# A linear attention in front of a mixture of experts: its instructions held to one fixed sequence

## The chip, the core and the metric

The kernel runs on one core of a Trainium2 chip. The core has five engines that run side by side, each through its own instructions in order: TensorE (PE, matrix multiplies), VectorE (DVE), ScalarE (ACT), GpSimd (POOL) and SyncE (SP), which here only starts DMA transfers. They meet through semaphores. Matrix products land in PSUM (eight banks), everything else lives in SBUF. The metric is the device time of one execution in microseconds (us); lower is better.

## What is computed

The reference is a linear attention followed by a mixture of eight experts with a balanced (Sinkhorn) gate, all in float32:

```python
# attention: q, k, v are (4 batches, 8 heads, 576, 64), omega is (128, 64)
def phi(x):
    proj = einsum('bhsd,md->bhsm', x, omega)
    h = proj - sum(x * x, -1) / 2
    return exp(h - max(h, -1)) / sqrt(m)
q_p, k_p = phi(q * scale), phi(k * scale)
kv, z = einsum('bhsm,bhsd->bhmd', k_p, v), sum(k_p, axis=2)
x = einsum('bhsm,bhmd->bhsd', q_p, kv) / (einsum('bhsm,bhm->bhs', q_p, z)[..., None] + 1e-6)
# experts: x as (2304, 512), w_gate (512, 8), w1 (8, 512, 1024), w2 (8, 1024, 512)
P = exp(x @ w_gate - max);  8 times: rows to sum 1, columns to sum 1, times N / E
out = sum over e of P[:, e] * (relu(x @ w1[e]) @ w2[e])
```

## The kernel before

**Jobs.** The attention is cut into 36 jobs. A job takes half of the heads of 256 rows of a batch's keys or queries; the 64 rows left over in each batch are paired over two batches (`kr`, `qr`). A job transposes its rows (`tp`, copied to `th` by ACT for keys and by DVE for queries), projects them on omega (`pp`, 16 matmuls in the profile), takes the row maximum out of PSUM (DVE, `sqs`), adds the squared norm to it (`cn`), and exponentiates: half of the job by way of DVE and one ACT instruction (`ex<-ex`), the other half by four ACT instructions that take `cn` as bias (`ex<-pp,cn`). A key job then multiplies by the values (`kv`). A query job transposes its features (`qp`, copied to `qt` by ACT), multiplies by `kvs` (`np`), divides (`rd`, `xt`, DVE), and its rows become token tiles by another transpose (`xp`, copied to `xf` by ACT). The squared norms come from an ACT square (`sq`) and a tree of sums on POOL (`squares`, two buffers).

**Side work between the jobs.** When six token tiles (a chunk, three in all) are there, `token_operands` computes the gate logits (`lp`, `gp`) and seven operands `xs` of a Strassen product: sums on POOL (on DVE for the last chunk), a rounded copy by ACT, a residual by DVE, and a DMA that writes both to DRAM (`xd`). `xs` has a ring of four tiles. The first expert's weights are loaded by `stage` and cut by `split` into a rounded half `wh` (ACT) and a residual `wl`, in the attention on POOL.

**The order.** The program's text gives the work to a scheduler, which runs a timeline of its own and orders each engine's queue by it. A `tick` advances every job in flight by one stage. `ensure_loads` starts a value's load two jobs ahead and a key's or query's five; SP's queue takes all DMAs. To keep squares, staging and splits from being scheduled too early, eight columns of their buffers are first written by a POOL copy from the newest `cn` (`last_cn`), so that the real write has to wait for it. After the attention, the expert part runs `first` (hidden products, `hx`, `hz`) and `second` (output products, `x`, `z`, `w`) interleaved; the last chunk's operands are the first that it uses.

Of the kernel before, what the change touches and what calls it, by code (L numbers as in the profile page):

```python
# [22 lines left out]
def moe_attention_kernel(  # L23
# [67 lines left out]
    ORDER = [1, 5, 6, 3, 7, 2, 4]  # L91

# [6 lines left out]
    def token_operands(c, x):  # L99
# [7 lines left out]
        next(gate_steps)  # L107

        def sub(o, a, b):
            (nc.vector if last else nc.gpsimd).tensor_tensor(o, a, b, op=ALU.subtract)  # L110

        for i in ORDER:
            if i == 5:
                sub(q(0, 0), q(0, 1), q(0, 0))
            elif i == 6:
                sub(q(0, 0), q(1, 1), q(0, 0))
            elif i == 7:
                sub(q(0, 1), q(1, 1), q(0, 1))  # L120
            elif i == 4:
                sub(q(0, 0), q(1, 0), q(0, 0))
            o = {3: q(1, 1), 7: q(0, 1), 2: q(1, 0)}.get(i, q(0, 0))
# [45 lines left out]
    last_cn = []  # L169
# [14 lines left out]
    def split(u, w, i):  # L184
# [39 lines left out]
        wt[u, w, i] = (hi, lo)  # L224

# [32 lines left out]
    def load(which, key):  # L258
# [31 lines left out]
    def squares(which, key):  # L290
# [5 lines left out]
        if last_cn:  # L296
            nc.gpsimd.tensor_copy(s.rearrange("p h j d -> p (h j d)")[:, :8], last_cn[-1])
# [18 lines left out]
    def feature_stages(which, key, hh, on_act):  # L316


# [10 lines left out]
        yield  # L329
        hs = sqt[which, key].rearrange("p h j t -> p (h j) t")[:, 8 * hh : 8 * hh + 8]  # L330
# [45 lines left out]
    def k_job(key, hh):  # L376
        ex = yield from feature_stages("k", key, hh, True)
        vt = rawt["v", key]
        if key[0] == "r":

            for a in range(2):
                b, r = 2 * key[1] + a, slice(a * SR, (a + 1) * SR)
                for hg in range(2):
# [4 lines left out]
                    if a == 0:  # L388
                        kv_close(b, hg)
# [19 lines left out]
    def q_job(key, hh, t0):
        ex = yield from feature_stages("q", key, hh, True)  # L410
        qt = []
        for g in range(2):
# [3 lines left out]
            t = sc.tile([P, 4, P], F32, tag="qt", bufs=4, name="qt")  # L416
            nc.scalar.copy(t.rearrange("p a s -> p (a s)"), tp)
            qt.append(t)
        yield
        shared = key[0] == "r"  # L420
        nj = 1 if shared else 2
        if hh == 0:
            xts[key] = sc.tile([P, 2, H, D], F32, tag="xt", bufs=2, name="xt")
        xt = xts[key]
        rd = sc.tile([P, 2, 4, 1], F32, tag="rd", bufs=2, name="rd")
        nums = []
        for g in range(2):
            nps = bank("np")
            n3 = nps[:, : 4 * (D + 1)].rearrange("p (h d) -> p h d", h=4)
            nums.append(n3)  # L430
            for i, (h, j) in enumerate(slots(key, hh, g)):
                for a in range(2):
# [3 lines left out]
                        n3[r, i, :], lhsT=qt[g][:, i, r], rhs=kv[:, h], start=True, stop=True  # L436
                    )
            nc.vector.tensor_scalar_add(rd[:, g], n3[:, :, :1], 1e-6 * M)
        nc.vector.reciprocal(rd, rd)
        for g, n3 in enumerate(nums):  # L440
            o = xt[:, 0, g::2] if shared else xt[:, g, 4 * hh : 4 * hh + 4]
            nc.vector.tensor_tensor(o, n3[:, :, 1 : D + 1], rd[:, g].to_broadcast([P, 4, D]), op=ALU.mult)
        yield
        if not shared and hh == 0:
            return
        c, col = t0 // CT, t0 % CT * P
        if c not in xf:
            xf[c] = sc.tile([P, KD, CL], F32, tag="xf", bufs=2, name="xf")
        for j in range(nj):
            xps = bank("xp")  # L450
            xj = xt[:, j].rearrange("p h d -> p (h d)")
            for kk in range(KD):
                nc.tensor.transpose(xps[:, kk * P : (kk + 1) * P], xj[:, kk * P : (kk + 1) * P], ident)
# [399 lines left out]
```

## Time and profile before

| | us |
|---|---|
| median of 3 runs (1633.61 to 1635.28) | 1633.7 |
| the profiled execution's own time | 1634.42 |
| its span, first to last instruction | 1632.6 |
| busy PE, DVE, ACT, POOL in the span | 1584.5, 1379.9, 777.3, 312.4 |
| mean granted clock of PE | 0.994 |

The span is what the engines' rows cover, and the execution's own time lies some 2 us above it. PE's weight loads (PEld) run beside its matmuls and are counted apart. A granted clock of 1.00 is 2.4 GHz; a mean below it holds some time at 1.2 GHz. Times in the rows below count from the span's start.

### The profile page before, as it was taken

The page shows a single profiled execution, that of the slowest core. Times are in us where ns is not written, and L with a number is a line of the kernel's source. Part 1 is how long each engine was busy: PE and PEld are TensorE (multiplying, and loading weights), DVE is VectorE, ACT ScalarE, POOL GpSimd, SP SyncE. Part 2 cuts the span into 40 slices and gives each one's busy share as a digit, 9 for nine tenths or more (in the row PEclk, how much of TensorE's full clock was granted, in tenths as well). Part 3 has the DMA queues.
Part 4 walks back from the last instruction along what each step waited for, and adds up shares of the span by engine and source line. Part 5 has one row for each costly group of instructions (what it writes and reads, how often), then busy time and mean ns, then how long its engine had stood idle before and what let it go on. Part 6 is the DMA issues. An engine that isn't in the chain of part 4 may idle for free.

```text
span 1632.6 us, 31484 instructions
## 1 busy us (share of the span) xinstructions
PE 1584.5 (97%) x12318; PEld 1551.6 (95%) x12318; DVE 1379.9 (85%) x2714; ACT 777.3 (48%) x1396; POOL 312.4 (19%) x340
## 2 busy tenths in 40 slices
PE   7899799999999999999999999999999999999998
PEld 5778699999999999999999999999999999999997
DVE  3788888998888898989888888989898888889777
ACT  5788654544434444534444444434344444444333
POOL 5585230111111010201111111102011111110003
PEclk9999999999999999999999999999999999999999
DMA  9442866666656565666565665656666556655562
GB/s 237 122 157 73 329 246 216 216 208 218 201 195 213 186 221 198 222 204 232 204 219 197 203 217 179 229 193 229 203 220 218 205 197 206 213 178 192 181 226 77
DMA packets 105315, 329.80 MB, mean 202 GB/s; under 512 B 14800, under 2 KB 43984, under 8 KB 105168
## 3 DMA queue, kind: packets, MB, share of 16 engines
q1 hardware_dynamic: 105168, 327.79, 59.5%
q8 instruction: 98, 1.61, 0.4%
q14 instruction: 49, 0.40, 0.1%
HBM read 306.53 MB, written 21.23 MB: 201 GB/s over the span
## 4 chain that ended last, share of the span: by engine, by line
PE 86%; DVE 7%; ACT 2%; POOL 2%; DMA 2%; issue 1%; SPq 0%; DVEq 0%; ACTq 0%; POOLq 0%
PE hx L549 24%; PE x L650 23%; PE hz L549 18%; PE z L650 11%; PE w L650 6%; PE pp L335 2%; DVE out L676 1%; DVE sm L586 1%; POOL sq L302 1%; DVE bl L586 1%; DVE sqs L338 1%; PE kv L360 1%; DVE xs L126 1%; ACT ex L348 0%; DMA xs<-xd 0%
## 5 line engine op out<-in xcount | busy, mean ns | idle before, releaser
L549 PE MATMUL hx<-xs,wh 128*128 128x384 f32 x1536 | 374.3, 337 | 2.0 <-ACT xs L125 1.4
L676 DVE SCALAR_TENSOR_TENSOR out<-x,prob,out 128x256 f32<-128x256 f32 x497 | 233.3, 476 | 65.8 <-PE x L650 64.3
L549 PE MATMUL hz<-xs,wh 128*128 128x384 f32 x1152 | 281.5, 336 | 2.1 <-ACT xs L125 1.1
L549 PEld LDWEIGHTS hx<-xs,wh 128*128 128x128 f32 x1536 | 270.1, 189 | 3.5 <-issue 3.2
L190 POOL TENSOR_TENSOR st<-st 128x512 f32<-128x512 f32 x80 | 131.7, 1646 | 700.1 <-DVE wl L223 697.1
L549 PEld LDWEIGHTS hz<-xs,wh 128*128 128x128 f32 x1152 | 202.4, 188 | 2.9 <-issue 1.3
L549 PE MATMUL hx<-xs,wl 128*128 128x384 f32 x768 | 199.4, 337 | 0.0
L628 ACT ACTIVATE bh<-hr 128x512 fp32r<-128x512 f32 x144 | 91.2, 634 | 222.0 <-PE x L650 217.0
L676 DVE SCALAR_TENSOR_TENSOR out<-z,prob,out 128x256 f32<-128x256 f32 x252 | 120.0, 476 | 58.0 <-PE z L650 57.2
L222 ACT CAST wh<-st 128x512 fp32r<-128x512 f32 x176 | 105.1, 621 | 110.9 <-PE hx L549 44.8
L624 ACT CAST sh<-sm 128x512 fp32r<-128x512 f32 x144 | 89.7, 623 | 139.9 <-PE z L650 100.1
L549 PE MATMUL hz<-xs,wl 128*128 128x384 f32 x576 | 150.1, 335 | 0.0
L549 PEld LDWEIGHTS hx<-xs,wl 128*128 128x128 f32 x768 | 138.9, 189 | 0.0
L586 DVE SCALAR_TENSOR_TENSOR sm<-hr,sm 128x256 f32<-128x256 f32 x288 | 133.5, 464 | 2.7
L223 DVE TENSOR_TENSOR wl<-st,wh 128x512 fp32r<-128x512 f32 x169 | 119.7, 719 | 11.6 <-ACT wh L222 11.1
L586 DVE SCALAR_TENSOR_TENSOR bl<-hr,bh 128x512 fp32r<-128x512 f32 x144 | 118.2, 821 | 3.1 <-ACT bh L628 1.5
L650 PE MATMUL z<-wh,sh 128*128 128x256 f32 x576 | 117.9, 281 | 2.8 <-ACT sh L607 2.7
L650 PE MATMUL x<-wl,sh 128*128 128x256 f32 x576 | 118.4, 282 | 0.0
L650 PE MATMUL x<-wh,sh 128*128 128x256 f32 x576 | 117.3, 284 | 0.7 <-DVE out L676 0.6
L598 ACT ACTIVATE ah<-hr 128x256 fp32r<-128x256 f32 x144 | 60.3, 419 | 120.6 <-PE x L650 98.9
L650 PE MATMUL z<-wh,sl 128*128 128x256 f32 x576 | 115.5, 282 | 1.6 <-DVE sl L608 1.6
L650 PE MATMUL z<-wl,sh 128*128 128x256 f32 x576 | 116.8, 281 | 0.0
(153 smaller groups left out, 3481.6 us busy)
## 6 DMA issues: line engine op xcount, KB each, us to landing
xs<-xd SPq DMA_DIRECT2D x329, 768.0 KB, 4.4
st<-in_moe_w_dram SPq DMA_DIRECT2D x64, 512.0 KB, 4.9
xd<-xs SPq DMA_DIRECT2D x21, 768.0 KB, 3.8
k<-in_k_dram SPq DMA_DIRECT2D x8, 512.0 KB, 6.5
v<-in_v_dram SPq DMA_DIRECT2D x8, 512.0 KB, 6.5
q<-in_q_dram SPq DMA_DIRECT2D x8, 512.0 KB, 6.2
out_dram<-out SPq DMA_DIRECT2D x32, 128.0 KB, 1.9
kr<-in_k_dram SPq DMA_DIRECT2D x4, 128.0 KB, 6.4
```

What stands on the lines that cost most here:

```text
L126: nc.vector.tensor_tensor(t[:, 1], o, raw(t[:, 0]), op=ALU.subtract)
L190: nc.gpsimd.tensor_tensor(o, a, b, op=op)
L222: nc.scalar.copy(hi, o)
L223: (nc.vector if u > 0 or (w == 2 and i in (1, 6, 7, 4)) else nc.gpsimd).tensor_tensor(lo, o, raw(hi), op=ALU.subtract)
L335: nc.tensor.matmul(pp[g][:, i * M : (i + 1) * M], lhsT=th[r, i], rhs=omt[r], start=True, stop=True)
L549: nc.tensor.matmul(pb, lhsT=a[:, k, g * P : (g + 1) * P], rhs=x[:, b, k, :], start=i in (1, 5, 2) and j == 0, stop=j == len(prods) - 1, sk ...
L586: nc.vector.scalar_tensor_tensor(o, in0=a, scalar=0.0, in1=b, op0=ALU.max, op1=op)
L598: nc.scalar.activation(ah, a11, AF.Relu)
L624: nc.scalar.copy(sh, sm)
L628: nc.scalar.activation(bh, a[:, 1:], AF.Relu)
L650: nc.tensor.matmul(pb, lhsT=ops[s][i][a][:, f], rhs=wt[u, 2, i][b][:, f], start=bool(start) and j == 0, stop=j == len(prods) - 1, skip_gro ...
L676: nc.vector.scalar_tensor_tensor(o, in0=pb, scalar=p, in1=o, op0=ALU.mult, op1=ALU.add)
```

## The change

The attention is written as one sequence. `feature_stages`, `k_job` and `q_job`, generators that the old `tick` advanced, become small functions (`transposes`, `projections`, `maxima`, `shifts`, `exps`, `keys_by_values`, `query_transposes`, `query_copy`, `numerators`, `quotients`, `token_transposes`, `token_copy`) that the new `tick(j)` calls in one order for the jobs j + 1, j, j - 1 and j - 2. What it traces is collected, and at the end every instruction gets an ordering edge (without a semaphore) to the one before it on its engine; SP's DMAs are among them. The expert part gets no edges. The copies from `last_cn` are gone. Loads are asked for eight jobs ahead, in order of use, and a value three jobs later than its key. The token operands of chunks 0 and 1 and the first weight splits follow written plans, a part each half tick (`s` is a sum, `c` a cast, `l` a residual); the sums of chunk 1 go into value buffers that are free by then, no longer over the tokens, and the first weights' residuals `wl` move from POOL to DVE. The first weights are staged at job 7 instead of 16, the second at job 32 instead of 30, the shared query job `qr(0)` goes from the middle to the end, `kvs` has 4 buffers instead of 3, `qr` 2 instead of 1 and `ex` 6 instead of 8. No arithmetic is added to the attention or the experts. The diff, cut to its core:

```diff
@@ token_operands @@
+        if c == 0:
+            at = {i: {3: q(1, 1), 7: q(0, 1), 2: q(1, 0)}.get(i, q(0, 0)) for i in ORDER}
+            plan = "|c1 |c3 l1.s5|c2 l3|c5 l2.s7| l5.s6|c7 |c6 l7| l6.s4| |c4 | l4|"
+        else:
+            at = {1: q(0, 0), 3: q(1, 1), 2: q(1, 0)}
+            for n, i in enumerate((5, 6, 7, 4)):
+                at[i] = vts[n].rearrange("p h c -> p (h c)")[:, : 2 * HL].rearrange("p (k t) -> p k t", k=2)
+            plan = "|s5.c1.c3 s7.l1|c2 l3.s6|c5 l2.s4|c7 l5|c6 l7|c4 l6.l4|"
...
@@ stage, split, squares @@
-            if u == 0:
-                nc.gpsimd.tensor_copy(t[:, 0, 0, :8], last_cn[-1])
...
-        if u == 0 and w == 1:
-            nc.gpsimd.tensor_copy(hi[:, 0, :8], last_cn[-1])
...
-        if last_cn:
-            nc.gpsimd.tensor_copy(s.rearrange("p h j d -> p (h j d)")[:, :8], last_cn[-1])
@@ first_splits (new) @@
+        for step in "|s5.c1 | l1|c2 |c5 l2| l5.s6.s7| |c4 |c6 l4|c7 l6.s3| l7| |c3 | l3|".split():
+            for part in step.split("|"):
+                for what in part.split(".") if part else ():
...
+                    if what[0] == "s":
+                        a, b, op = sums[i]
+                        nc.gpsimd.tensor_tensor(at[i], a, b, op=op)
+                    elif what[0] == "c":
...
+                        nc.scalar.copy(hi, at[i])
+                        wt[0, 1, i] = (hi, lo)
+                    else:
+                        hi, lo = wt[0, 1, i]
+                        nc.vector.tensor_tensor(lo, at[i], raw(hi), op=ALU.subtract)
+                yield
@@ the driver @@
     def ensure_loads(i):
-        for it in list(need):
-            if it[0] <= (i + 2 if it[1] == "v" else i + 5):
-                need.remove(it)
-                load(it[1], it[2])
...
+        while need and need[0][0] <= i + 8:
+            _, w, key = need.pop(0)
+            load(w, key)
...
+    def tick(j):
...
+        now, nxt = job(j), job(j + 1)
+        while closing:
+            kv_close(*closing.pop(0))
+        if now:
+            projections(now)
+            maxima(now, 0)
+        ensure_squares(j)
+        if nxt:
+            transposes(nxt)
+        tps = []
+        if job(j - 1, "q"):
+            tps = query_transposes(job(j - 1))
+            for t in tps:
+                query_copy(job(j - 1), *t)
+        if now:
+            maxima(now, 1)
+            shifts(now)
+            exps(now, 1)
+        go_on()
+        for xt, i, t in turned[: 1 if j < 28 else None]:
+            turned.pop(0)
+            token_copy(token_transposes(xt, i, t), t)
+        if now:
+            exps(now, 0)
+        for it in leftover:
+            next(it, None)
+        leftover.clear()
+        if job(j - 2, "q"):
+            numerators(job(j - 2))
+        if job(j - 1, "k"):
+            it = keys_by_values(job(j - 1))
+            next(it)
+            leftover.append(it)
+        if job(j - 2, "q"):
+            quotients(job(j - 2))
+        go_on()
...
+    in_order = mybir.DependencyInfo(mybir.DependencyClass.NoSync, mybir.DependencyReason.DATA)
+    before = {}
+    for ins in pinned:
+        if ins.engine in before:
+            tc.add_manual_dep(ins, before[ins.engine], in_order, reason="order of the attention")
+        before[ins.engine] = ins.name
```

**The first jobs.** ACT's queue from job 0's exponentials on, before and with the change (the numbers tell buffers apart; `sq_218` is the square of the keys that jobs 5 and 7 use):

```order
L348 ACTIVATE ex_163<-pp_147,cn_158 128x128 x4
L298 ACTIVATE sq_177<-kr_112 128x512
L351 ACTIVATE ex_160<-ex_160 128x512
L326 COPY th_215<-tp_210 128x512
L348 ACTIVATE ex_205<-pp_189,cn_200 128x128 x4
L298 ACTIVATE sq_218<-k_115 128x1024
L351 ACTIVATE ex_202<-ex_202 128x512
```

```order
L419 ACTIVATE ex_171<-pp_140,cn_168 128x128 x4
L415 ACTIVATE ex_170<-ex_170 128x512
L377 COPY th_196<-tp_191 128x512
L419 ACTIVATE ex_202<-pp_181,cn_199 128x128 x4
L415 ACTIVATE ex_201<-ex_201 128x512
L349 ACTIVATE sq_239<-kr_111 128x512
L377 COPY th_254<-tp_249 128x512
```

Each square stood between a job's four exponentials and its last one; it now stands behind the last one. POOL's queue at the start, before and with the change (the last row of before is a copy from `cn`):

```order
L302 TENSOR_TENSOR sq_117<-sq_117 128x16x4
L302 TENSOR_TENSOR sq_127<-sq_127 128x16x32
L302 TENSOR_TENSOR sq_117<-sq_117 128x16x2
L302 TENSOR_TENSOR sq_127<-sq_127 128x16x16
L303 TENSOR_TENSOR sqs_118<-sq_117 128x16
L302 TENSOR_TENSOR sq_127<-sq_127 128x16x8
L304 TENSOR_SCALAR sqs_118<-sqs_118 128x16
L302 TENSOR_TENSOR sq_127<-sq_127 128x16x4
L297 COPY sq_177<-cn_158 128x8
```

```order
L353 TENSOR_TENSOR sq_122<-sq_122 128x16x4
L353 TENSOR_TENSOR sq_122<-sq_122 128x16x2
L354 TENSOR_TENSOR sqs_123<-sq_122 128x16
L355 TENSOR_SCALAR sqs_123<-sqs_123 128x16
L353 TENSOR_TENSOR sq_150<-sq_150 128x16x32
L353 TENSOR_TENSOR sq_150<-sq_150 128x16x16
```

The second tree ran inside the first one; it now follows it, and the copies from `cn` are gone.

**Chunk 0's operands.** DVE's queue around jobs 22 to 24, before and with the change (`xs` are the residuals of token operands, `wl` one of the weights):

```order
L126 TENSOR_TENSOR xs_1705<-xf_834,xs_1705 128x768
L338 TENSOR_REDUCE sqs_1254<-pp_1674 128x4
L126 TENSOR_TENSOR xs_1786<-xf_834,xs_1786 128x768
L338 TENSOR_REDUCE sqs_1254<-pp_1675 128x4
L328 COPY th_1701<-tp_1696 128x512
L126 TENSOR_TENSOR xs_1879<-xf_834,xs_1879 128x768
L126 TENSOR_TENSOR xs_1942<-xf_834,xs_1942 128x768
L340 TENSOR_REDUCE cn_1686<-sqs_1254 128x8
L338 TENSOR_REDUCE sqs_1308<-pp_1749 128x4
L350 TENSOR_TENSOR ex_1688<-pp_1674,cn_1686 128x512
L126 TENSOR_TENSOR xs_2029<-xf_834,xs_2029 128x768
```

```order
L123 TENSOR_TENSOR xs_1549<-xf_833,xs_1549 128x768
L399 TENSOR_REDUCE sqs_1272<-pp_1743 128x4
L379 COPY th_1759<-tp_1754 128x512
L399 TENSOR_REDUCE sqs_1272<-pp_1744 128x4
L404 TENSOR_REDUCE cn_1776<-sqs_1272 128x8
L406 TENSOR_TENSOR ex_1778<-pp_1743,cn_1776 128x512
L123 TENSOR_TENSOR xs_1646<-xf_833,xs_1646 128x768
L276 TENSOR_TENSOR wl_1692<-t_842,wh_1691 128x512
```

Five residuals stood within one and a half jobs; now one stands behind each job's `ex`, and a `wl` joins some of them. The query copy `th` goes from behind both maxima to between them.

**The handover.** PE's queue at the first output products (`ah` and `sh` are their left operands), before and with the change:

```order
L650 MATMUL x<-wh,al 128x256 x2
L650 MATMUL z<-wh,sh 128x256 x2
L650 MATMUL z<-wl,sh 128x256 x2
L467 MATMUL mt<-ident,m_3071 1x128
L650 MATMUL z<-wh,sl 128x256 x2
L650 MATMUL x<-wh,sh_2952 128x256 x2
L549 MATMUL hx<-xs,wh 128x384 x2
```

```order
L751 MATMUL x<-wh,al 128x256 x2
L650 MATMUL hx<-xs,wh 128x384 x2
L650 MATMUL hx<-xs,wl 128x384 x2
L650 MATMUL hx<-xs,wh 128x384 x4
L650 MATMUL hx<-xs,wl 128x384 x2
L650 MATMUL hx<-xs,wh 128x384 x2
L751 MATMUL z<-wh,sh 128x256 x2
```

The twelve `hx` products that came after `sh` now come ahead of it.

## Rows read from the trace of the kernel before

**Rows 1.** By stage: us, busy us of PE PEld DVE ACT POOL, PEclk, DMA, GB/s.

```profile
7.57:48.88 41.31, 32.18 (x477) 27.46 (x477) 20.75 (x42) 25.62 (x62) 25.32 (x58) 0.96 1.11 230
48.88:93.99 45.11, 42.13 (x700) 36.99 (x697) 36.17 (x88) 38.16 (x96) 27.32 (x66) 1.00 0.34 95
93.99:121.76 27.77, 24.82 (x322) 20.81 (x319) 24.18 (x46) 22.43 (x47) 24.70 (x27) 0.88 0.56 210
121.76:157.08 35.32, 33.55 (x533) 29.63 (x533) 29.87 (x76) 29.56 (x77) 18.08 (x36) 1.00 0.18 62
157.08:175.73 18.65, 13.84 (x187) 9.79 (x187) 13.00 (x29) 13.05 (x26) 7.28 (x4) 1.00 0.52 208
175.73:208.00 32.27, 25.03 (x130) 23.04 (x131) 26.32 (x39) 18.12 (x32) 11.29 (x7) 0.89 0.80 320
208.00:1610.00 1402.00, 1395.30 (x9856) 1388.15 (x9855) 1215.04 (x2373) 620.18 (x1045) 185.23 (x121) 1.00 0.61 207
```

**Rows 2.** Waits of ACT, 0 to 50 us: us in total, times, longest.

```profile
ACT sq L298 <- POOL sq L297: 5.5, 4, 1.6
ACT sq L298 <- DMA k<-in_k_dram: 1.9, 1, 1.9
```

**Rows 3.** Timeline of PE: start, us, engine, line, operation [idle before <-releaser].

```profile
25.42 1.69 PE L360 MATMUL kv<-v,ex 128*64 128x65 f32 x32 [2.43 <-ACT ex L351]
...
53.75 1.15 PE L435 MATMUL np<-kvs,qt 128*64 128x65 f32 x32
54.74 1.10 PE L360 MATMUL kv<-v,ex 128*64 128x65 f32 x32
55.77 1.16 PE L335 MATMUL pp<-omt,th 64*128 64x128 f32 x16
56.86 0.66 PE L323 MATMUL tp<-ident,q 128*128 128x128 f32 x4
...
109.61 1.16 PE L335 MATMUL pp<-omt,th 64*128 64x128 f32 x8 [1.28 <-DVE th L328]
...
173.48 0.63 PE L453 MATMUL xp<-ident,xt 128*128 128x128 f32 x4 [2.13 <-DVE xt L442]
...
198.53 0.51 PE L650 MATMUL z<-wh,sh 128*128 128x256 f32 x2 [2.67 <-ACT sh L607]
```

**Rows 4.** Timeline of ACT, 23 to 25 and 67 to 70 us.

```profile
23.79 1.06 ACT L298 ACTIVATE sq<-q 128x1024 f32<-128x1024 f32 x1 [1.44 <-POOL sq L297]
...
67.24 1.16 ACT L348 ACTIVATE ex<-pp,cn 128x128 f32<-128x128 f32 x4
68.25 0.67 ACT L351 ACTIVATE ex<-ex 128x512 f32<-128x512 f32 x1
68.77 0.62 ACT L326 COPY th<-tp 128x512 f32<-128x512 f32 x1
```

**Rows 5.** Timeline of POOL, 5 to 25 us.

```profile
6.89 2.99 POOL L302 TENSOR_TENSOR sq<-sq 128x512 f32<-128x512 f32 x4 [5.13 <-ACT sq L298]
...
19.66 3.32 POOL L302 TENSOR_TENSOR sq<-sq 128x512 f32<-128x512 f32 x5 [1.17 <-ACT sq L298]
...
23.37 0.27 POOL L304 TENSOR_SCALAR sqs<-sqs 128x16 f32<-128x16 f32 x1
```

**Rows 6.** Timeline of DVE, 13, 94 and 109 us.

```profile
13.51 0.18 DVE L340 TENSOR_REDUCE cn<-sqs 128x8 f32<-128x24 f32 x1 [2.54 <-POOL sqs L304]
...
94.74 0.96 DVE L126 TENSOR_TENSOR xs<-xf,xs 128x768 fp32r<-128x768 f32 x1 [0.15 <-ACT xs L125]
...
109.48 3.84 DVE L126 TENSOR_TENSOR xs<-xf,xs 128x768 fp32r<-128x768 f32 x2
```

**Rows 7.** The page's costliest groups, weight residuals: count | busy, mean ns.

```profile
L223 DVE TENSOR_TENSOR wl<-st,wh 128x512 fp32r<-128x512 f32 x169 | 119.7, 719 | 11.6 <-ACT wh L222 11.1
```

**Rows 8.** Groups of DVE by form, 0 to 176 us.

```profile
L126 DVE TENSOR_TENSOR xs<-xf,xs 128x768 fp32r<-128x768 f32 x13 | 17.5, 1361 | 4.8 <-ACT xs L125 4.7
```

**Rows 9.** The chain that ended last, 174 to 205 us: start, us, what.

```profile
184.66 5.20 DMA xd<-xs
```

More of the change, by code (lines that the diff above doesn't have):

```diff
@@ L106, in token_operands, with total, cast, low @@
         gate_steps = logits(c, x)
[L107 to L123, printed above, removed]
+        if last:
+            next(gate_steps)
+        def total(o, i, s):
+            eng = nc.vector if last else nc.gpsimd
+            a, b = {5: (q(0, 1), s), 6: (q(1, 1), s), 7: (q(1, 1), q(0, 1)), 4: (q(1, 0), s)}[i]
+            eng.tensor_tensor(o, a, b, op=ALU.subtract)
+        def cast(i, o):
             t = token_tile()
             nc.scalar.copy(t[:, 0], o)
+            return t
+        def low(i, o, t):
             nc.vector.tensor_tensor(t[:, 1], o, raw(t[:, 0]), op=ALU.subtract)
@@ L128, in token_operands @@
             nc.sync.dma_start(out=xdram[c, i], in_=raw(t))
-            if last:
+        if last:
+            for i in ORDER:
+                n = len(traced)
+                o = {3: q(1, 1), 7: q(0, 1), 2: q(1, 0)}.get(i, q(0, 0))
+                if i in (5, 6, 7, 4):
+                    total(o, i, o)
+                t = cast(i, o)
+                low(i, o, t)
+                pinned.extend(traced[n:])
                 xop[0, c, i] = t
@@ L314, in slots, with transposes @@
         return [(4 * hh + i, g) for i in range(4)]
-    def feature_stages(which, key, hh, on_act):
+    def transposes(jb):
+        which, key, hh = jb[:3]
         tin = rawt[which, key].rearrange("p h j d -> p (h j d)")
@@ L403, in k_job, with query_transposes @@
         if last:
-            kv_close(b, hh)
+            closing.append((b, hh))
         yield
+    closing = []
     xts = {}
[L409 to L412, printed above, removed]
+    def query_transposes(jb):
+        ex = exs.pop(jb)
+        tps = []
+        for g in (1, 0):
             tp = bank("qp")
@@ L447, in q_job, with token_transposes @@
+    turned = []
+    def token_transposes(xt, j, t):
+        c = t // CT
         if c not in xf:
             xf[c] = sc.tile([P, KD, CL], F32, tag="xf", bufs=2, name="xf")
[L449 to L453, printed above, removed]
-            cs = slice(col + j * P, col + (j + 1) * P)
-            nc.scalar.copy(xf[c][:, :, cs], xps.rearrange("p (k s) -> p k s", k=KD))
-            yield
@@ L457, in q_job, with token_copy @@
-        done_q[c] += nj
-        if done_q[c] == CT:
-            yield from token_operands(c, xf[c])
+        xps = bank("xp")
+        xj = xt[:, j].rearrange("p h d -> p (h d)")
+        for kk in range(KD):
+            nc.tensor.transpose(xps[:, kk * P : (kk + 1) * P], xj[:, kk * P : (kk + 1) * P], ident)
+        return xps
+    def token_copy(xps, t):
+        c, col = t // CT, t % CT * P
+        nc.scalar.copy(xf[c][:, :, col : col + P], xps.rearrange("p (k s) -> p k s", k=KD))
+        done_q[c] += 1
+        if done_q[c] == CT:
+            it = token_operands(c, xf[c])
+            if c < NCH - 1:
+                next(it)
+                extra.append(it)
+            else:
+                at_last.append(it)
@@ L462, in sinkhorn @@
+    extra, at_last = [], []
     def sinkhorn():
@@ L758, in moe_attention_kernel @@
+    begin = len(traced)
+    ensure_loads(0)
+    ensure_squares(-1)
+    for i in range(-1, len(jobs)):
+        if i == 7:
+            stage(0, 1)
+            prepare_gate()
+        if i == 12:
+            it = first_splits()
+            next(it)
+            extra.append(it)
+        if i == 32:
             stage(0, 2)
-        gen = k_job(jb[1], jb[2]) if jb[0] == "k" else q_job(*jb[1:])
-        active.append((jb, gen))
-        tick()
+        tick(i)
         ensure_loads(i + 1)
-    tick()
+    for i in range(len(jobs), len(jobs) + 3):
+        tick(i)
```

179 lines of the change are left out of this document (110 added, 69 removed).

## The prediction, made before the run

> **What bounds the kernel now.** I read the busy time by stage first [rows 1]. From 208 to 1610 us, the expert part, TensorE (PE) is busy 1395.3 of 1402.0 us, and the change pins nothing there. What can move is the attention and the handover before 208 us. I cut them at starts of projections (`pp`, one group of 16 matmuls per job, 36 jobs): A is jobs 0 to 8 (41.31 us), B jobs 9 to 20 (45.11), C jobs 21 to 25 (27.77), D jobs 26 to 34 (35.32), E from the last job's projections to the first expert matmul (18.65), F from there to 208 us (32.27). PE is busy for 93% of B, but 78% of A, 89% of C at a mean granted clock of 0.88, 74% of E, and 78% of F at 0.89 (below 1.00 means that part of the stretch ran at 1.2 instead of 2.4 GHz). So the losses sit in A, C, E and F; B shows what an undisturbed mix of jobs costs, 3.76 us per job.
>
> Why A is slow shows in the waits of the first 50 us [rows 2] and in the engines' rows. ScalarE (ACT) stood 5.5 us, four times, behind the 8-column copies on GpSimd (POOL) that tie a square's buffer to the newest `cn`. The square stands ahead of the exponential that `kv` needs: the square at 23.79 waited 1.44 us, and the `kv` behind it made PE wait 2.43 us until 25.42 [rows 3, 4]. Earlier, POOL ran four of the first square's sums, then began the second square's tree inside the first's, so that the first `cn` waited for POOL until 13.51 [rows 5, 6]. C is slow because the seven token operands of chunk 0 were issued nearly together: two `xs` residuals on VectorE (DVE) took 3.84 us at 109.48, the query copy that PE needed came just ahead of them and late, and PE waited 1.28 us until 109.61 [rows 3, 6]; after that the clock fell.
>
> **The change, term by term.** PE's own sequence hardly changes (in both orders: project, transpose the next job, then query transposes or numerators and `kv`), so what is priced is when ACT, DVE and POOL let it go on.
>
> *A, jobs 0 to 8.* One tree alone takes 4.0 us (from 19.66 to the end of the row at 23.37), so one that starts at 6.89 ends at 10.9, and `cn` comes at 10.95 instead of 13.51 [rows 5, 6]. I keep the slow PE durations of the first two jobs as they are and move job 2 forward by 1.5 us, the part of these 2.5 that PE, itself busy with jobs 0 and 1, can use: it projects at 16.4 (17.9 before). A key job then costs PE, by its row 0.66 (`tp`) and by the steps between starts 1.03 (`kv`) + 1.09 (`pp`), together 2.8 [rows 3], and ACT 1.01 + 0.52 + 0.62 = 2.15 (four exponentials, one more, `th`), with a square of 1.06 3.2 [rows 4]. Every second or third tick has a square; with a hop or two I take 3.1 for each of jobs 2 to 4, so job 5 projects at 25.7. Jobs 5 to 8 cost PE 2.8, 3.8, 2.8 and 3.8 (numerators 0.99, query transposes taken at the same), together 13.2, and 0.4 for hops: job 9 at 39.3, and A is 31.7 us long. I take 33, a gain of 8.3. Bounds: 4 (only most of the 5.5 us of [rows 2] comes back) and 9.6 (the walk as it stands).
>
> *B, jobs 9 to 20.* Most of the first weight splits are now cast here, and their residuals move from POOL to DVE. DVE gains 5 of the 7 inside B at 0.72 each [rows 7], 3.6 us, and goes from 36.17 to 40; ACT gains about 6 casts at 0.62, the row of a copy of the same 128x512 [rows 4], 3.7 us, and goes from 38.16 to 42; PE has 42.13 [rows 1]. They are hidden while each engine stays within PE's time, but with little slack left. I take 46, a loss of 0.9; bounds 43 and 49. The query copy moved between the two maxima costs nothing; it frees PE earlier. The 1 MB of first weights is issued at job 7 instead of 16 and stands ahead of later keys, values and queries in the only queue; those are asked for eight jobs ahead, some 25 us, and 512 KB takes 2.3 us at A's 230 GB/s [rows 1], so I cost it at nothing. If that cover failed it would be the 4.6 us of the two loads.
>
> *C, jobs 21 to 25.* At full clock PE's work is about 24.82 - 0.12 x 27.77 = 21.5 [rows 1]. Of six token residuals of 1.36 [rows 8], four stay at about 1.2, spread over ticks, and two `wl` come: DVE 24.18 - 8.2 + 4.8 + 1.4 = 22.2. I take 22.8, for two engines at that level: a gain of 5.0. Bounds 2 (spread, but the clock still falls) and 6.
>
> *D, jobs 26 to 34.* Here work arrives: three residuals of chunk 0 and one or two of chunk 1 (DVE 29.87 + 5 x 1.2 = 36), and chunk 1's gate logits with some token transposes come over, about 2.5 of the 13.84 us of PE work in E (PE 33.55 + 2.5 = 36) [rows 1]. I take 38.5, a loss of 3.2; bounds 35 and 42.
>
> *E, from the last projections to the first expert matmul.* The chain is maxima, shift, exponentials, query transposes, copies, numerators, quotients, token transposes, their copy, gate logits. Before, DVE had residuals in pairs ahead of the quotients, and PE waited 2.13 us for `xt` until 173.48 [rows 3]. The order now lets one through per step, and two jobs are still in flight behind the last. Without the second residual of each pair I get 15.5, a gain of 3.1; bounds 13 and 18.65 (nothing).
>
> *F, the handover.* Chunk 1's writes begin earlier and no longer stand between chunk 2's: the chain shows 5.20 us for such a write ahead of a cast [rows 9]. PE also stood 2.67 us for `sh` until 198.53 [rows 3]; the new order has twelve `hx` matmuls in that place, about 2.1 us. I take 29.5, a gain of 2.8; bounds 27 and 34 (the same DVE chain, reached with the ring of four `xs` tiles fuller).
>
> *Expert part.* The scheduler reorders it in detail, with nothing added or removed: 0, give or take 1.5.
>
> A rule bears on the residuals. Measured first: one took 0.96 us at 94.74 and two took 3.84 at 109.48 [rows 6], while POOL ran sums. The Trainium skill ("SBUF — State Buffer", "Who interferes with whom") says that a VectorE instruction with two SBUF inputs and a GpSimd instruction that reads SBUF exclude each other for the whole instruction. These rows agree with it. By that rule a residual that meets POOL work doubles, and the seven that move from POOL to DVE would meet the squares' trees; that is the second rival.
>
> Sum: 8.3 - 0.9 + 5.0 - 3.2 + 3.1 + 2.8 = 15.1. The profiled execution took 1634.4 us (its span is 1632.6), 0.7 above the median of 1633.7: 1634.4 - 15.1 = 1619.3, or 1618.6 against the median. I say **1619**.
>
> **Rivals.**
> 1. *The start is bound by loads.* For: the DMA engines' share was 1.11 throughout A [rows 1]. Against: ACT waited only 1.9 us for a key load in the first 50 us [rows 2]. Were it so, A would give 2 instead of 8.3: 1625. Chance 0.10.
> 2. *Residuals held up by POOL.* If 21 residuals took 1.9 instead of 1.2 or 0.72, DVE would have some 19 us more; after my sum B, C and D leave DVE about 10 us of slack, so 8 or 9 end on the path: 1627. For: the pair at 109.48 [rows 6]. Against: POOL loses its seven `wl` and the tie copies, and was busy for only 18.08 of the 35.32 us of D [rows 1]. Chance 0.13.
> 3. *More than I count.* F keeps the clock up, pairs in B lose their waits for `ex`, and all terms come out near their upper bounds: 1608. Chance 0.12.
> 4. *The change doesn't do what it says.* PE's sequence was nearly this one already; if the new order of ACT and DVE only trades waits, the time is within 3 us of 1634. Chance 0.07.
> 5. *Slower.* The fixed order ties ACT into a ring with PE: last exponential of a query job, query transposes and copy, key exponentials, square, `th` copy, query exponentials. By [rows 3, 4] that is 0.5 (half the transposes) + 0.6 + 1.0 + 0.5 + 1.06 + 0.6 + 1.0 + 0.5 = 5.8 us per pair of jobs, up to 2 us of casts and token copies stand in it, and B's pair takes 7.5. If hops add 1.5 us, a pair takes 9.0, and the 13 pairs of B to D lose 20 us, against 15 won: 1639. It decides from a pair of 8.7 us on. For: an ACT that waits now holds up everything behind it. Against: before, pairs ran at 7.5 us with the same copies ahead of the same exponentials. Chance 0.08.
>
> **How the numbers follow.** My forecast (its own range 1613 to 1625) has 0.50. A difference of 0.2%, 3.3 us, is about what a measurement of this kernel can tell from no change. Faster by more: 0.50 + 0.10 + 0.13 + 0.12 = 0.85; the same 0.07; slower 0.08. The range 1610 to 1631 leaves out the fourth and fifth rivals and the far half of the third, 0.2 in all.
>
> **What the new profile would show.** The projections of job 9 near 41 us (48.88 before), of job 21 near 87 (93.99), of job 26 near 109 (121.76), of job 35 near 148 (157.08), the first expert matmul near 163 (175.73), PE steady from some 193 (208). No square that waits for POOL in the first 50 us; token residuals of 0.96 to 1.3 us, one per tick; PE's clock at 1.00 from job 21 to 26. I am wrong if ACT waits for query transposes on every second job, if pairs in B exceed 7.8 us, or if the last chunk's casts still wait some 5 us for writes of `xs`.

## The result, and the profile after

The changed kernel takes 1614.0 us (median of 4 runs, 1611.28 to 1614.47), the kernel before 1633.7 beside it: a ratio of 0.9875, 95% interval 0.9858 to 0.9892, some 20 us less. I had forecast 1619. The profiled execution of the changed kernel (1611.28, span 1609.4) lies 2.7 us below its median and that of the kernel before 0.7 above its own, so the stages below add up to 23.2 us, 3.5 more than the medians differ by; that much is luck.

The stages of the new profile, cut at the same projections as in [rows 1] (the sixth row covers as long a stretch behind the first expert matmul as F did). Columns as there.

```profile
7.54:38.47 30.93, 28.84 (x477) 24.80 (x477) 20.62 (x41) 24.20 (x60) 22.67 (x50) 1.00 0.93 215
38.47:80.51 42.04, 41.24 (x699) 36.71 (x696) 38.65 (x96) 40.05 (x99) 27.70 (x49) 1.00 0.65 152
80.51:101.64 21.13, 20.22 (x343) 16.87 (x339) 18.94 (x39) 19.23 (x46) 14.44 (x20) 1.00 0.35 113
101.64:140.73 39.09, 36.90 (x542) 30.85 (x539) 37.14 (x85) 34.48 (x84) 27.04 (x37) 1.00 0.54 184
140.73:154.87 14.14, 10.93 (x164) 7.84 (x160) 11.58 (x31) 10.44 (x21) 1.54 (x1) 1.00 0.61 245
154.87:187.14 32.27, 26.21 (x141) 24.23 (x142) 26.38 (x37) 17.79 (x32) 10.97 (x7) 0.95 0.85 333
```

| stage | before | forecast | after | gain, forecast | gain, measured |
|---|---|---|---|---|---|
| A | 41.31 | 33 | 30.93 | 8.3 | 10.4 |
| B | 45.11 | 46 | 42.04 | -0.9 | 3.1 |
| C | 27.77 | 22.8 | 21.13 | 5.0 | 6.6 |
| D | 35.32 | 38.5 | 39.09 | -3.2 | -3.8 |
| E | 18.65 | 15.5 | 14.14 | 3.1 | 4.5 |
| first expert matmul to the end | 1456.87 | 1454.1 | 1454.53 | 2.8 | 2.3 |
| sum | | | | 15.1 | 23.2 |

PE is now busy in 93% of A and 98% of B. ScalarE's waits of the first 50 us hold no square that waits for POOL any more, as [rows 2] did:

```profile
ACT th L377 <- PE tp L374: 4.0, 3, 2.1
ACT L289 <- DMA om<-in_omega_dram: 3.3, 1, 3.3
ACT qt L492 <- PE qp L485: 1.9, 3, 1.2
ACT ex L419 <- DVE cn L404: 1.6, 3, 1.1
```

PE's rows that answer to [rows 3], from its timeline (start, us, what, and the wait before it):

```profile
11.34 2.08 PE L389 MATMUL pp<-omt,th 64*128 64x128 f32 x16 [0.68 <-ACT th L377]
...
15.63 1.16 PE L389 MATMUL pp<-omt,th 64*128 64x128 f32 x16
...
152.70 0.63 PE L544 MATMUL xp<-ident,xt 128*128 128x128 f32 x4 [1.38 <-DVE xt L528]
...
179.27 0.50 PE L751 MATMUL z<-wh,sl 128*128 128x256 f32 x2 [1.68 <-DVE sl L709]
180.80 0.51 PE L751 MATMUL x<-wh,sh 128*128 128x256 f32 x2 [1.03 <-ACT wh L246]
182.04 0.80 PE L751 MATMUL x<-wl,sh 128*128 128x256 f32 x2 [0.73 <-DVE wl L247]
```

The reader is to see that job 2 projects at 15.63 (17.9 before) and that the wait of 2.67 us for `sh` in the handover is gone. The wait for `sl` is not new; the kernel before had it behind that for `sh` (its waits of PE, 175 to 208 us):

```profile
PE z L650 <- DVE sl L608: 1.6, 1, 1.6
```

The waits for `wh` (1.03) and `wl` (0.73) behind it are new.

### The profile page after: what moved, and what is told of

It is laid out like the page before. It is cut to its first block, busy times and chain, and to the rows that moved or that the text cites. A ratio compares the mean times of both kernels' runs of the same rounds, so it can differ in the third digit from the quotient of the medians.

```text
span 1609.4 us, 31434 instructions
## 1 busy us (share of the span) xinstructions
PE 1574.7 (98%) x12318; PEld 1543.1 (96%) x12318; DVE 1388.4 (86%) x2721; ACT 774.8 (48%) x1396; POOL 298.1 (19%) x304
## 4 chain that ended last, share of the span: by engine, by line
PE 86%; DVE 10%; ACT 2%; POOL 1%; issue 1%; DMA 0%; SPq 0%; DVEq 0%; ACTq 0%
PE hx L650 24%; PE x L751 23%; PE hz L650 18%; PE z L751 12%; PE w L751 6%; DVE sm L687 2%; DVE out L777 2%; PE pp L389 1%; DVE bl L687 1%; DVE sqs L399 1%; DVE wl L247 1%; POOL sq L353 1%; DVE sl L726 1%; PE tp L374 1%; DVE xs L123 1%
## 5 line engine op out<-in xcount | busy, mean ns | idle before, releaser
L216 POOL TENSOR_TENSOR st<-st 128x512 f32<-128x512 f32 x79 | 126.3, 1598 | 702.6 <-DVE wl L247 698.1
L246 ACT CAST wh<-st 128x512 fp32r<-128x512 f32 x172 | 102.9, 620 | 104.6 <-PE hx L650 43.9
L687 DVE SCALAR_TENSOR_TENSOR sm<-hr,sm 128x256 f32<-128x256 f32 x288 | 137.1, 476 | 2.6
L751 PE MATMUL x<-wh,sl 128*128 128x256 f32 x576 | 117.2, 282 | 0.0
```

Of the source, the lines that this page charges most:

```text
L216: nc.gpsimd.tensor_tensor(o, a, b, op=op)
L687: nc.vector.scalar_tensor_tensor(o, in0=a, scalar=0.0, in1=b, op0=ALU.max, op1=op)
L751: nc.tensor.matmul(pb, lhsT=ops[s][i][a][:, f], rhs=wt[u, 2, i][b][:, f], start=bool(start) and j == 0, stop=j == len(prods) - 1, skip_gro ...
```

## The experiments

Stages are named as above; each run's time is a median of four or five, with a kernel before timed beside it at 1634.2 to 1634.6, and its stages are those of its profiled execution.

**e1: no edges.**

```diff
-    for ins in pinned:
+    for ins in []:
```

> The changed kernel without its ordering edges: same text, same plans, same buffers, but the scheduler orders each queue. Theory of the fixed order (the edges themselves let TensorE run its stream without waits): stages A to E give back most of the 20.8 us they won, A over 35 us (30.9 with edges), B near 45 (42.0), and the time is 1626 to 1634. Rival, the pieces (ties gone, plans, more buffers, earlier loads do it, and the edges only write down what the scheduler would do anyway): A 31 to 32, B 42 to 43, time 1613 to 1617.

Measured: 1657.9 us, ratio 1.0147 (1.0133 to 1.0161): slower than the kernel before by 24 us. A 60.0, B 44.7, C 27.5, D 44.7, E 14.6. Both theories had it wrong in size: the text without its edges is not even the kernel before. ScalarE's and GpSimd's timelines show why A is so long:

```profile
29.57 0.62 ACT L272 CAST wh<-st 128x512 fp32r<-128x512 f32 x1 [6.53 <-DMA st<-in_moe_w_dram]
...
31.28 1.27 POOL L268 TENSOR_TENSOR t<-st 128x512 f32<-128x512 f32 x1 [4.34 <-DMA st<-in_moe_w_dram]
```

The scheduler put casts and sums of the first weights, meant for job 12 on, ahead of exponentials and trees of the first jobs, and both engines stood until that load had landed.

**e2: the kernel before without the ties of its squares.**

```diff
-        if last_cn:
-            nc.gpsimd.tensor_copy(s.rearrange("p h j d -> p (h j d)")[:, :8], last_cn[-1])
```

> The kernel before with one thing taken out: the eight-column copies on GpSimd that tie each square's buffer to the newest cn. If the ties are what made the start slow (ScalarE stood 5.5 us behind them, four times), A falls from 41.3 to 36 to 38 us and the time to 1629 to 1631. Rival, the place of the square (between a job's four exponentials and its last one) and the mixing of two trees on GpSimd cost it: A stays at 40 to 42 and the time at 1632 to 1636.

Measured: 1647.3 us, ratio 1.0083 (1.0069 to 1.0096); A 54.7 (41.3 with the ties). Neither theory foresaw that. ScalarE's timeline:

```profile
34.14 1.06 ACT L296 ACTIVATE sq<-k 128x1024 f32<-128x1024 f32 x1 [7.62 <-DMA k<-in_k_dram]
...
41.12 1.06 ACT L296 ACTIVATE sq<-k 128x1024 f32<-128x1024 f32 x1 [2.93 <-POOL sqs L301]
```

Squares of later jobs now stand ahead of this job's exponentials and wait for loads and trees. ScalarE waited 5.5 us behind the ties [rows 2], and without them A is 13.4 us longer.

**e5: the new text with the old ties, without edges.** The edges out as in e1, and:

```diff
+            if u == 0:
+                nc.gpsimd.tensor_copy(t[:, 0, 0, :8], last_cn[-1])
...
+                        nc.gpsimd.tensor_copy(hi[:, 0, :8], last_cn[-1])
...
+        if last_cn:
+            nc.gpsimd.tensor_copy(s.rearrange("p h j d -> p (h j d)")[:, :8], last_cn[-1])
```

> The changed kernel's text and plans without the ordering edges, but with the eight-column GpSimd copies of the kernel before back on the squares, the first weights' tiles and their rounded halves. The run without edges and without ties took 1657.9 us, with A at 60.0. If the ties alone hold the squares back well enough and the new text and plans bring the rest (theory of the pieces): A 31 to 34, B 42 to 43, time 1613 to 1620. If the edges are what pays (theory of the fixed order), this is the kernel before with small changes: A 37 to 42, B 44 to 46, time 1628 to 1638.

Measured: 1642.3 us, ratio 1.0056 (1.0044 to 1.0069); A 41.0, B 50.4, D 46.5. The plans, buffers and early loads without the order cost 8 us; with it they come with a gain of 20. The theory of the pieces is out.

**e8 and e9: edges on some engines.**

```diff
     for ins in pinned:
+        if ins.engine != mybir.EngineType.Activation:
+            continue
         if ins.engine in before:
```

That is e8; e9 has `if ins.engine not in (mybir.EngineType.Activation, mybir.EngineType.Pool)` in its place.

> The changed kernel with ordering edges on ScalarE's instructions alone; the other engines' queues are the scheduler's. If it is ScalarE's order (squares, copies, casts among the exponentials) that pays, A is 31 to 33 and the time 1613 to 1620. If GpSimd's or VectorE's order counts as much (trees mixed into each other, residuals ahead of maxima), A is 35 to 45 and the time 1622 to 1640.

> The changed kernel with ordering edges on ScalarE and GpSimd alone. With edges on ScalarE alone, GpSimd stood 10.6 us before a sum of the first weights whose load had not landed, with the trees of the squares behind it, and A took 44.3 us. If that sum was what the other queues' freedom cost in A, A is back at 30 to 33 and the time falls by some 12 us to 1624 to 1629, with B to D still 2 to 8 us above those of the changed kernel. If the queues of VectorE, TensorE and the DMA queue cost as much again in A: A above 36, time over 1632.

Measured: e8 1639.6 us, ratio 1.0036 (1.0022 to 1.005), A 44.3, B 44.6, C 26.4, D 42.6; e9 1625.0, ratio 0.9944 (0.9931 to 0.9956), A 29.7, B 44.6, C 25.0, D 42.8. In e8 one sum on GpSimd held A, as the timelines of GpSimd, ScalarE and VectorE show:

```profile
31.55 1.26 POOL L268 TENSOR_TENSOR t<-st 128x512 f32<-128x512 f32 x1 [10.63 <-DMA st<-in_moe_w_dram]
...
37.73 1.06 ACT L349 ACTIVATE sq<-k 128x1024 f32<-128x1024 f32 x1 [8.93 <-POOL sqs L354]
...
38.08 0.18 DVE L404 TENSOR_REDUCE cn<-sqs 128x8 f32<-128x24 f32 x1 [7.71 <-POOL sqs L355]
```

The sum waits for a load, the trees stand behind it, and square and `cn` wait for a tree. Pinning GpSimd's queue as well took 14.6 us off, nearly all of it in A (about 1.5 us of A's fall is a quicker start, see the last section). The last 11 us, from e9 to the full set, lie in B to E, where PE waits for VectorE (its waits in e9, 37 to 150 us):

```profile
PE pp L389 <- DVE cn L404: 4.3, 4, 1.9
PE pp L389 <- DVE th L379: 3.8, 5, 1.7
PE pp L389 <- DVE ex L406: 1.3, 1, 1.3
```

That points at VectorE's order, but does not show it: an edge set on VectorE apart from PE's and SP's was not tried.

**e4: the square between the exponentials.**

```diff
-        ensure_squares(j)
         if nxt:
             transposes(nxt)
...
             exps(now, 1)
+        ensure_squares(j)
         go_on()
```

> The changed kernel with each square traced between a job's four exponentials and its last one, as it stood before, edges kept and no ties. If the place of the square matters, a product of keys and values comes 1.06 us later in every tick with a square: A grows by 2 to 4 us (to 33 to 35), B by 0.5 to 2, time 1617 to 1620. If only the ties mattered, the square is hidden there too: A 31 to 31.5, time 1613 to 1615.

Measured: 1621.1 us, ratio 0.9926 (0.9913 to 0.994), so 7 us given back: A 32.6, B 44.3, D 43.9, and 2.3 us behind the first expert matmul. The place of the square counts, less in A than I expected and more in D, which I had not named. There PE waits for quotients, query copies and exponentials, and its granted clock has a mean of 0.92. The window of D:

```profile
105.77:149.67 43.90, 39.17 (x542) 33.06 (x538) 39.11 (x85) 34.59 (x83) 27.81 (x37) 0.92 0.45 152
```

**e6: chunk 0's operands bunched.**

```diff
-            plan = "|c1 |c3 l1.s5|c2 l3|c5 l2.s7| l5.s6|c7 |c6 l7| l6.s4| |c4 | l4|"
+            plan = "c1.c3.c2|l1.l3.l2.s5 c5|l5.s7.s6 c7.c6|l7.l6.s4 c4|l4"
```

> The changed kernel with the seven operands of chunk 0 issued in bunches of up to three casts and three residuals per half tick instead of about one, edges kept. If bunching is what cost C its time before: the residuals hold up maxima and query copies, C 24 to 27 with the granted clock below 1.00 again, time 1617 to 1620. If the fixed order hides it (TensorE has its other job in flight): C 21 to 22, time 1613 to 1615.

Measured: 1619.1 us, ratio 0.9908 (0.9895 to 0.9922); C 29.2 (21.1), D 1.2 shorter. The medians differ by 5.1 us, the profiled executions, of which the stages are, by 9.3. The window of C, and rows of VectorE and PE inside it:

```profile
81.80:110.96 29.16, 23.25 (x343) 18.83 (x339) 23.78 (x44) 22.55 (x51) 19.68 (x22) 0.88 0.75 243
```

```profile
84.07 4.53 DVE L123 TENSOR_TENSOR xs<-xf,xs 128x768 fp32r<-128x768 f32 x3 [1.31 <-ACT xs L119]
...
86.09 0.66 PE L485 MATMUL qp<-ident,ex 128*128 128x128 f32 x4 [2.10 <-ACT ex L415]
...
89.27 2.04 PE L389 MATMUL pp<-omt,th 64*128 64x128 f32 x16
```

Three residuals take 4.53 us, PE waits, and its projection of 1.16 us takes 2.04: the mean clock of 0.88 that C had before [rows 1] is back. The one-per-tick plan is what C's gain rests on.

**e3: the first weights' residuals on GpSimd.**

```diff
-                        nc.vector.tensor_tensor(lo, at[i], raw(hi), op=ALU.subtract)
+                        nc.gpsimd.tensor_tensor(lo, at[i], raw(hi), op=ALU.subtract)
```

> The changed kernel with the seven residuals of the first weights back on GpSimd, edges kept. If B is bound by TensorE alone, 5 us less of work on VectorE there buy nothing: B 41.8 to 42.5 and the time 1613 to 1616. If VectorE's residuals held B or C back (the rival of the shared port), B or C gets shorter by 1 to 3 us: 1610 to 1612. If GpSimd with some 10 us more work makes the squares' trees late, cn waits for it and B grows by 2 to 5 us: 1616 to 1619.

Measured: 1612.9 us, ratio 0.987 (0.9857 to 0.9884), not to be told from the changed kernel; B 41.89, C 21.14. VectorE's load in B (38.65 us in the changed kernel) is not what sets it, and the move of the residuals neither cost nor gained.

**e7: the casts of the first weights twice.**

```diff
                         nc.scalar.copy(hi, at[i])
+                        nc.scalar.copy(hi, at[i])
```

> The changed kernel with each of the seven rounded copies of the first weights made twice by ScalarE (the second overwrites the first with the same values). Five of them lie in B, 0.71 us each, 3.5 us more for a ScalarE that is busy 40.05 of B's 42.04 us. If the casts are hidden behind TensorE (B is set by TensorE's own 41.2 us): B 42.0 to 42.6, time 1613.5 to 1615. If ScalarE is as much the bound as TensorE: B grows by what goes beyond the 2 us of slack or more, 43.5 to 45.5, time 1615.5 to 1618. My forecast (46 for B, with the casts once) would have had 47 and more.

Measured: 1616.6 us, ratio 0.989 (0.9876 to 0.9903). The window of B, where ScalarE has 2.9 us more to do (42.97 against 40.05):

```profile
37.05:81.94 44.89, 42.16 (x700) 36.85 (x696) 40.41 (x96) 42.97 (x104) 28.11 (x52) 1.00 0.61 142
```

B grows by 2.85 us. PE's waits in B, the one of the changed kernel and then the largest two new ones of e7, are all for ScalarE:

```profile
PE pp L389 <- ACT th L377: 0.8, 3, 0.3
```

```profile
PE qp L486 <- ACT ex L416: 1.1, 2, 0.6
PE np L510 <- ACT xf L551: 0.6, 2, 0.4
```

So the casts are hidden once, and not twice: at 40.05 of 42.04 us ScalarE is next to being the bound. Some of the 2.85 may be the execution: e12, whose attention is that of the changed kernel, shows 42.69 in B.

**e10: transposes ahead of the first work.**

```diff
+    idle = bank("idle")
+    for _ in range(11):
+        nc.tensor.transpose(idle[:, :P], ident, ident)
```

> The changed kernel with eleven extra transposes of the identity on TensorE ahead of its first real work, into a bank that nobody reads. TensorE was busy without gaps from 9.55 to 15.63 us with matmuls at twice their later duration (2.08 us for projections that later take 1.16). If the clock comes up earlier for it, jobs 0 and 1 project in 1.16, job 2 projects at 13.5 to 14.3 (15.63 in the profile of the changed kernel), and the time is 1611.5 to 1613. If the slow matmuls have another cause, or the start hangs on loads: job 2 at 15.5 or later, time 1613.5 to 1615.

Measured: 1612.7 us, ratio 0.9867 (0.9851 to 0.9882), not to be told from the changed kernel, and its PE rows say that nothing changed (in the changed kernel TensorE was not busy without gaps from 9.55 us, as I have it above; it stood 0.68 us ahead of the projection at 11.34):

```profile
1.54 2.61 PE L288 MATMUL idle<-ident 128*128 128x128 f32 x11 [1.54 <-POOL v L311]
...
11.49 2.08 PE L394 MATMUL pp<-omt,th 64*128 64x128 f32 x16 [0.68 <-ACT th L382]
...
16.02 1.16 PE L394 MATMUL pp<-omt,th 64*128 64x128 f32 x16
```

**e11: the last numerators ahead of the token transposes.**

```diff
+        if j > len(jobs) and job(j - 2, "q"):
+            numerators(job(j - 2))
         for xt, i, t in turned[: 1 if j < 28 else None]:
...
-        if job(j - 2, "q"):
+        if j <= len(jobs) and job(j - 2, "q"):
             numerators(job(j - 2))
```

> The changed kernel with one piece moved: in the step after the last two, the last numerators stand ahead of the token transposes of the job before, which wait for its quotients, instead of behind them. TensorE waited 1.38 us twice there, with the numerators queued behind the first wait. If E is this chain, E falls from 14.14 to 12.0 to 12.8 and the time to 1612 to 1613. If the residuals on VectorE or the copies on ScalarE set the end of E anyway: E 13.8 to 14.5, time 1613.5 to 1615.

Measured: 1614.1 us, ratio 0.9875 (0.9862 to 0.9888); E 14.50 (14.14). The numerators come earlier, but the last token transposes then wait for a ScalarE cast instead of for `xt`:

```profile
150.22 0.63 PE L544 MATMUL xp<-ident,xt 128*128 128x128 f32 x4 [0.45 <-DVE xt L528]
152.26 0.94 PE L544 MATMUL xp<-ident,xt 128*128 128x128 f32 x4 [1.41 <-ACT xs L119]
```

**e12: GpSimd's part of the handover on VectorE.** The sums and residuals of the first unit's second weights:

```diff
-            nc.gpsimd.tensor_tensor(o, a, b, op=op)
+            (nc.vector if (u, w) == (0, 2) else nc.gpsimd).tensor_tensor(o, a, b, op=op)
...
-        (nc.vector if u > 0 or (w == 2 and i in (1, 6, 7, 4)) else nc.gpsimd).tensor_tensor(lo, o, raw(hi), op=ALU.subtract)
+        nc.vector.tensor_tensor(lo, o, raw(hi), op=ALU.subtract)
```

> The changed kernel with the sums and residuals of the second weights of the first unit on VectorE instead of GpSimd, so that GpSimd does nothing while the first hidden products are turned into operands; the scheduler reorders the expert part around it, the attention is untouched. In the changed kernel's handover VectorE's sm, bl and al take 2.93 us for two, 1.78 and 1.50 us while GpSimd runs those sums, and 0.87, 0.83 and 0.42 beside nothing. If the two engines hold each other up there, these instructions fall to their short durations, TensorE waits less before 183 us, and the part from the first expert matmul on gets 1 to 3 us shorter: time 1611 to 1613. If the lengths are VectorE's own, or the 5 us of work that come to VectorE cost as much as is won: that part is the same or 1 to 3 us longer, 1614 to 1617.

Measured: 1607.6 us (1606.41 to 1609.66), ratio 0.9834 (0.9817 to 0.9851), faster than both kernels. First the changed kernel, VectorE and GpSimd:

```profile
171.86 3.08 POOL L216 TENSOR_TENSOR st<-st 128x512 f32<-128x512 f32 x2 [29.59 <-DVE wl L247]
...
172.04 1.78 DVE L687 SCALAR_TENSOR_TENSOR bl<-hr,bh 128x512 fp32r<-128x512 f32 x1
173.74 2.93 DVE L687 SCALAR_TENSOR_TENSOR sm<-hr,hn 128x256 f32<-128x256 f32 x2
176.59 1.50 DVE L687 SCALAR_TENSOR_TENSOR al<-hr,ah 128x256 fp32r<-128x256 f32 x1
```

And e12, VectorE:

```profile
172.22 0.69 DVE L687 SCALAR_TENSOR_TENSOR bl<-hr,bh 128x512 fp32r<-128x512 f32 x1
...
173.42 0.76 DVE L687 SCALAR_TENSOR_TENSOR sm<-hr,hn 128x256 f32<-128x256 f32 x2
...
174.69 0.42 DVE L687 SCALAR_TENSOR_TENSOR al<-hr,ah 128x256 fp32r<-128x256 f32 x1
```

The same four instructions take 6.21 us beside GpSimd's sums and residual and 1.87 without them (the 0.83 us that I expected for `bl` alone stands in no row; it is 0.69). PE by stretch in the handover, the changed kernel and then e12:

```profile
172.00:182.04 10.04, 5.38 (x33) 4.55 (x31) 9.99 (x15) 6.46 (x13) 6.34 (x5) 1.00 1.00 391
182.04:185.50 3.46, 3.46 (x12) 3.46 (x13) 0.88 (x2) 0.72 (x3) 3.46 (x3) 0.51 0.32 133
```

```profile
172.00:182.04 10.04, 8.22 (x55) 7.80 (x55) 10.04 (x22) 8.67 (x18) 0.00 (x0) 1.00 1.01 394
182.04:185.50 3.46, 3.46 (x25) 3.46 (x25) 1.58 (x5) 1.84 (x4) 0.00 (x0) 1.00 1.00 365
```

In the first stretch VectorE does 22 instructions instead of 15, PE's work goes from 33 to 55 matmuls, and the clock no longer falls to 1.2 GHz (0.51) behind it. From the first expert matmul to the end e12 takes 1450.1 us instead of 1454.5. The scheduler also reordered the rest of the expert part, but these 4.4 us are won in the handover. For 18.13 us from the first expert matmul on, both kernels do 94 matmuls; the next 12.50 us are, in the changed kernel and then in e12:

```profile
173.00:185.50 12.50, 7.83 (x37) 7.01 (x37) 9.88 (x15) 6.97 (x15) 8.80 (x7) 0.86 0.81 325
```

```profile
172.60:185.10 12.50, 10.68 (x71) 10.26 (x70) 10.62 (x24) 9.89 (x20) 0.00 (x0) 1.00 1.00 391
```

There e12 gets 34 matmuls ahead, which at the 0.14 us that one takes behind it are some 4.8 us, and it gains nothing more in the 1420 us that follow. What of this VectorE's new order there adds to its shorter instructions was not separated.

## Why the prediction was right, and where it was too small

**The direction and its cause.** Faster was right, but the reason in my text was incomplete: I named the places (squares, bunched residuals), and left open that the order itself has to hold them there. With the text unchanged, no edges gives 1657.9, ScalarE alone 1639.6, with GpSimd 1625.0, all engines 1614.0. The edges carry 44 us, or 28 where the old ties stand in for them (e5: 1642.3); without them the new text is slower than the kernel before. What the pieces of the text are worth under the edges was tried for the squares' place (7 us, e4), the plan of chunk 0 (5 us, e6) and the residuals' engine (nothing, e3). The larger rings, the earlier loads and edges on the old text were not tried apart, so their shares are not shown.

**A, 8.3 forecast, 10.4 measured.** The walk over PE's rows was right (31.7 against 30.93); the 1.3 us that I added on top was not needed, and job 2 came 0.8 earlier than its 16.4, with the first `cn` at 11.06 us for the 10.95 that I had. What I read wrongly was the tie: 5.5 us of waiting behind it looked like a cost to be taken away, and e2 shows that taking it away alone makes A 13.4 us longer. It paid because edges hold the squares in its stead: in e9, with edges on ScalarE and GpSimd alone and no ties, A is 29.7 us.

**B, a loss of 0.9 forecast, a gain of 3.1 measured.** This is the term that was most off, by 4.0 us and outside its bounds of 43 to 49. The step that failed is "I take 46, a loss of 0.9", where I let three engines at 40 to 42 us cost 4 us of friction. PE waits 0.8 us in all of B, and pairs run at 6.6 to 7.6 us. ScalarE came out at 40.05 us, 2 below my 42: five casts lie there, not six, e7 shows that five add 2.9 us, not five times a row's 0.7, and a token operand's cast of 0.93 us that stood in B before is gone from it. How near the bound it is, e7 shows: with 2.9 us more on it B grows to 44.89. The order, not the text alone, makes it: without edges, or with those of ScalarE and GpSimd, B is 44.6 to 44.7 (50.4 in e5).

**C, 5.0 forecast, 6.6 measured.** The mechanism was right: the clock is 1.00 throughout, and e6 brings both the 0.88 and the time back. The size was not: PE's work there came out at 20.22 us, not the 21.5 that I took from [rows 1], and its waits at 0.9, not 1.3. VectorE had 18.94 us to do, not 22.2: three token residuals stayed in C, not four, of seven before, not six.

**D and E.** D at 39.09 against 38.5: the work that arrives is as counted (PE 36.9, VectorE 37.1, 36 forecast for each). E at 14.14 against 15.5, its bound 13; e11 shows that the next thing behind PE's wait for `xt` is a cast on ScalarE.

**F and the expert part, 2.8 forecast, 2.3 measured.** As sized, but not quite by the steps that I named: the twelve products do fill the wait of 2.67 for `sh`, yet of the 4.3 us that PE stood for `sh` and `sl` before, 3.4 come back as waits for `sl` (1.68), `wh` (1.03) and `wl` (0.73), and its clock falls to 0.51 for 3.46 us. I had not seen what delays VectorE there, its instructions beside GpSimd's; the kernel before has it too (two `sm` took 2.90 us, `bl` 1.65), and e12 shows what it costs.

**The marks.** Forecast and found: job 9 near 41, 38.47; job 21 near 87, 80.51; job 26 near 109, 101.64; job 35 near 148, 140.73; the first expert matmul near 163, 154.87; PE steady from 193, from about 185.5. No square waits for POOL in the first 50 us, and the clock is 1.00 from job 21 to 26. The token residuals in C took 0.97, 1.44 and 1.78 us, not 0.96 to 1.3. Of the signs of error, none showed in full: pairs in B stay below 7.8 us, the last chunk's casts wait 1.7 us at most, not 5, and ScalarE waits for query transposes 4 times in the 12 jobs of B, 1.3 us in all, not in every second.

**The rivals.** A bound by loads is out: A gained 10.4. No effect is out. The ring that ends slower is out: it would have had B to D lose 20 us, and they take 102.3 together, against 108.2 before. "More than I count" (1608) came half true: A, B and C passed their upper bounds, the handover did not. Residuals held up by GpSimd were a real mechanism in the wrong place: e3 shows that the seven that moved cost nothing, and the rows below that a residual that meets a tree can take longer. The Trainium skill ("SBUF — State Buffer", "Who interferes with whom") has the two engines exclude each other for such instructions; e12 agrees with it, with 6.21 against 1.87 us.

## What to carry to other kernels

A wait in the trace may be a guard: before an engine's 5.5 us behind a tie are counted as gain, ask what comes forward once it is gone. Where a scheduler misjudges when loads land, fix the order per engine, on the slow side engines too: here that was worth more (28 to 44 us) than the placements tried inside it (7 and 5). Look for a VectorE instruction at twice or four times its usual duration, and for GpSimd work beside it, wherever the matrix engine waits for VectorE.

## What the runs showed of the hardware

**VectorE and GpSimd hold each other up, and either may pay.** From the changed kernel's timelines of both, a residual beside a tree of five sums, twice:

```profile
88.67 3.92 POOL L353 TENSOR_TENSOR sq<-sq 128x512 f32<-128x512 f32 x5 [5.54 <-ACT sq L349]
88.98 1.78 DVE L123 TENSOR_TENSOR xs<-xf,xs 128x768 fp32r<-128x768 f32 x1
...
94.98 4.65 POOL L353 TENSOR_TENSOR sq<-sq 128x512 f32<-128x512 f32 x5
98.56 0.97 DVE L123 TENSOR_TENSOR xs<-xf,xs 128x768 fp32r<-128x768 f32 x1
```

At 88.98 the residual takes 1.78 us instead of 0.96, the median of its kind in that kernel. At 98.56 it takes 0.97, and the tree beside it 4.65 instead of 3.32 [rows 5]; an earlier residual (at 94.40, 1.44 us) also lies over that tree's start.

**The first matmuls run at half pace for a varying time.** The first projections take 2.08 us, later ones 1.16, while the granted clock in the profile reads 1.00. In e7, e9 and e12 the second job already projects in 1.16 and A takes 29.4 to 29.7 us; in the changed kernel and in e3, e10 and e11 it takes 2.08 there, and A 30.9 to 31.4. The row of e7, beside that of the changed kernel at 11.34 above:

```profile
11.46 1.16 PE L390 MATMUL pp<-omt,th 64*128 64x128 f32 x16 [0.68 <-ACT th L378]
```

TensorE's work and its sequence up to there are the same in e7, e9, e12 and the changed kernel, and 2.61 us of transposes ahead of it (e10) did not help. What decides it stays open; it is worth some 1.5 us.
